# Sliding-window attention into a Silu MLP: first layers of tiles 0 and 1 in all eight PSUM banks, the Silu table loaded behind batch 1's Exp, batch 1's values in the scores' banks

## The chip, the cores and the metric

The kernel runs on one core of one Trainium2 chip. The metric is device time in microseconds (us) for one launch, the median of several runs. Before the change it is 298.0 us over 11 runs, which lie between 296.94 and 300.13.

TensorE (PE) multiplies, and its weight loads are shown as PEld; VectorE (DVE) and ScalarE (ACT) read its results from PSUM; GpSimd (POOL) issues nearly all loads here; SyncE (SP) issues the stores. PSUM has eight banks of 128 partitions by 512 float32 numbers.

## The reference, cut to what matters

```python
# q, k, v: (8, 8, 576, 64) = batch, heads, sequence, head size
scores = scale * np.matmul(q, k.transpose(0, 1, 3, 2))
rel = pos[:, None] - pos[None, :]
mask = (rel >= 0) & (rel < 64)
scores = np.where(mask, scores, -1e9)
attn = softmax(scores)                       # exp, divided by the sum over keys
x = matmul(attn, v), heads side by side      # (4608, 512)
h = x @ w_in                                 # (512, 2048)
g = h * (1.0 / (1.0 + np.exp(-h)))           # Silu
out = g @ w_out                              # (2048, 512), float32
```

A query sees only itself and the 63 keys before it, so a block of 64 queries needs a window of 128 keys. The largest score need not be subtracted at these sizes, and the kernel does not subtract it.

## The kernel before, in words

**Attention.** A batch has 576 positions, nine blocks of 64. Batch 0 is done in six units of three blocks and half of the heads. Batches 1 to 7 are done in *visits* of three blocks (four from batch 2's seventh block on) over all heads (`add_visit`, L570). A visit is a chain over four engines: scores on PE into the four banks called `at` (`scores`, L326), four Exps on ACT that free these banks (`expo`, L343), four multiplications by a 0/1 mask on DVE (`masking`, L346), the values product on PE (`values`, L362, called pv below) into two banks, and for each of these on DVE a reciprocal (`inverse`), a multiplication (`normal`) and a transpose into the tile `bridge` (`to_bridge`). `bridge` holds the attention's output with the model dimension on the partitions, as the MLP wants it.

**MLP.** The 4608 tokens are nine tiles of 512. A tile's first layer makes 16 stripes `ft` of 128 hidden units: four matmuls (`first_layer`, L392) into one bank, then one Silu on ACT into an SBUF tile `g` (`silu`, L398). The second layer (`second_layer`, L404) accumulates 16 stripes into one bank per 128 tokens, then copies the bank to SBUF (`copy_out`, L410) and stores it (`store`, L413). Tile 0 takes all nine blocks of batch 0, 64 tokens more than it needs; `rest_of_first` (L401) copies their stripes over to tile 1. Tile 0's second layer goes stripe by stripe over four banks, so that it can follow the stripes of `w_out` as they land; the other tiles finish one bank after the other. Tile 1's first layer comes in two parts for 14 of its stripes: 192 tokens (batch 1's first visit), then 256 tokens (its second and third).

**The order of work.** No scheduler of the compiler orders this kernel. `Plan.run` (L47) is a list scheduler that runs when the kernel is built: each operation is put in a queue by its class (`add`, L28) with an estimated duration, the operations that it depends on, and a latency `lat` after which its result counts as seen (0.08 us if none is given). At every simulated moment each free engine takes, among the heads of its queues, the ready one with the lowest rank: the class's number plus the batch, or a number of its own for batch 0 (`rank0`, and `ahead` for classes whose name ends in 0). The order that results is each engine's instruction order on the chip, where an engine waits at each instruction for what it needs. A load on POOL counts as seen at its transfer's modelled end plus `lat` plus 1.2 us; no more than eight are under way. All loads after the first few share one queue, in the order in which they were added.

**Banks.** An operation that opens a bank takes it from a pool (L176): `at` is banks 0 to 3, `mp` banks 4 to 7, `pv` banks 4 and 5, `all` all eight. A bank is free once the operations in its `untils` list are seen. An operation of the pools `at`, `pv` or `all` that is ready but finds too few free banks keeps its pool from operations of higher rank number. Before the change the first layers open their banks in `mp`, batch 1's first visit puts its values in `at` and its second and third in `pv`. The gate `scores_may_run` (L426) lets whole visits' scores in only while the next MLP matmul is of a second layer with enough left.

**Activation tables.** The plan starts with Exp's table and charges 1.28 us for a change. An operation of class `prime` (L688) does one small Silu as soon as batch 0's Exps are done, so that the table is there for tile 0.

## Time and profile before

| | |
|---|---|
| median of 11 runs | 298.0 us |
| profiled execution: its own time | 299.71 us |
| profiled execution: span, first to last instruction | 297.9 us |
| PE busy (matmuls) | 285.0 us, 96% |
| ACT busy | 169.2 us, 57% |
| DVE busy | 141.8 us, 48% |
| POOL busy | 117.8 us, 40% |
| granted TensorE clock | 1.000 of full speed, mean |

The profiled execution took 1.8 us more than its span and 1.7 us more than the median. Busy time is a sum over a program whose stages differ: loads fill the first 60 us or so (the page's DMA row is at 8 or 9 tenths there), and PE is busy at nearly every moment afterwards. So the stages have to be read one by one. In a line of the timeline the columns are start in us, length in us, engine, source line, operation, destination and sources, and how many instructions were merged; a bracket tells the idle time before it and what ended it. In the chain the columns are start, length and what the time went to; "issue" there is time for which the profile names no wait.

### The profile page before, as it was taken

How to read it: one execution, taken by the hardware profiler on the slowest of the kernel's cores; microseconds unless marked ns; L12 is line 12 of the kernel's file. 1: busy time of each engine (PE TensorE's matmuls, PEld its weight loads, DVE VectorE, ACT ScalarE, POOL GpSimd, SP SyncE). 2: the span in 40 equal slices, each digit the busy share in tenths (PEclk: the TensorE clock that was granted, in tenths of full speed). 3: DMA queues.
4: the chain of work that ended last, by engine and by line, in shares of the span. 5: the costliest groups of instructions: out<-in, count | busy, mean ns of one | idle time of the engine just before them, and what ended most of it. 6: DMA issues, size and time to landing. Idle time of an engine off the chain costs nothing.

```text
span 297.9 us, 8490 instructions
## 1 busy us (share of the span) xinstructions
PE 285.0 (96%) x3611; PEld 150.5 (51%) x3641; DVE 141.8 (48%) x344; ACT 169.2 (57%) x316; POOL 117.8 (40%) x175
## 2 busy tenths in 40 slices
PE   7989977899999999999999999999999999999996
PEld 4567633685444554455544554455544444444445
DVE  3872377868894687837792891065504000000000
ACT  4878654786387636773487447654863157126511
POOL 8967894969799997980320000000000000000000
PEclk9999999999999999999999999999999999999999
DMA  8999999999999999994290120011100210010012
GB/s 167 173 188 181 149 155 151 226 142 132 160 178 136 118 163 173 157 108 94 52 111 0 37 75 35 1 37 64 49 0 4 96 42 2 35 70 35 3 70 72
DMA packets 82982, 28.64 MB, mean 96 GB/s; under 512 B 72448, under 2 KB 78208, under 8 KB 82944
## 3 DMA queue, kind: packets, MB, share of 16 engines
q0 software_dynamic: 77184, 18.07, 65.7%
q1 hardware_dynamic: 5760, 10.03, 9.4%
q8 instruction: 28, 0.46, 0.6%
q14 instruction: 10, 0.08, 0.1%
HBM read 36.70 MB, written 9.44 MB: 155 GB/s over the span
## 4 chain that ended last, share of the span: by engine, by line
PE 80%; DMA 8%; POOL 7%; issue 3%; ACT 1%; POOLq 0%; ACTq 0%
PE mp L393 30%; PE mp L405 29%; PE at L405 9%; PE at L393 6%; DMA w_out_sb<-in_moe_w_out_dram 5%; PE mp L368 3%; DMA w_in_sb<-in_moe_w_in_dram 3%; PE at L334 3%; POOL vv L255 2%; POOL w_in_sb L261 2%; POOL nat L241 1%; POOL natb L231 1%; POOL w_out_sb L267 0%; ACT ot L411 0%; ACT g L399 0%
## 5 line engine op out<-in xcount | busy, mean ns | idle before, releaser
L393 PE MATMUL mp<-bridge,w_in_sb 128*128 128x512 bf16 (+5 forms) x612 | 109.9, 337 | 2.6 <-ACT g L399 0.8
L405 PE MATMUL mp<-w_out_sb,g 128*128 128x512 bf16 x421 | 97.4, 379 | 5.3 <-DMA w_out_sb<-in_moe_w_out_dram 2.6
L393 PEld LDWEIGHTS <-w_in_sb 128*128 128x128 bf16 x696 | 66.6, 98 | 61.7 <-issue 3.1
L399 ACT ACTIVATE g<-mp 128x512 bf16<-128x512 f32 (+5 forms) x153 | 77.4, 513 | 26.5 <-PE mp L393 25.3
L405 PEld LDWEIGHTS <-g 128*128 128x128 bf16 x608 | 56.5, 98 | 65.3 <-issue 3.5
L344 ACT ACTIVATE e<-at 128x512 bf16<-128x512 f32 (+1 forms) x68 | 33.0, 572 | 16.3 <-PE at L334 16.2
L241 POOL DMA_DIRECT2D nat<-in_k_dram x56 | 34.7, 633 | 13.8 <-DMA vv<-in_v_dram 6.5
L255 POOL DMA_DIRECT2D vv<-in_v_dram x32 | 32.0, 1018 | 14.1 <-PE mp L368 12.4
L411 ACT COPY ot<-mp 128x512 f32<-128x512 f32 x20 | 11.6, 587 | 44.8 <-PE mp L405 22.6
L241 POOL DMA_DIRECT2D nat<-in_q_dram x56 | 35.0, 644 | 2.9 <-DMA w_in_sb<-in_moe_w_in_dram 1.5
L375 DVE RECIPROCAL rc<-mp 128x6 f32<-128x6 f32 (+1 forms) x47 | 7.9, 185 | 49.4 <-PE mp L368 48.8
L405 PE MATMUL at<-w_out_sb,g 128*128 128x512 bf16 (+2 forms) x157 | 28.2, 336 | 0.2
L248 DVE STREAM_TRANSPOSE kt<-nat 128x576 bf16<-128x576 bf16 x28 | 20.7, 786 | 7.5 <-DMA nat<-in_k_dram 7.5
L349 DVE TENSOR_TENSOR e<-e,masks 128x512 bf16<-128x512 bf16 (+1 forms) x68 | 23.3, 392 | 1.5 <-ACT e L344 1.2
L248 DVE STREAM_TRANSPOSE qt<-nat 128x576 bf16<-128x576 bf16 x28 | 21.0, 792 | 3.8 <-DMA nat<-in_q_dram 3.7
L378 DVE TENSOR_TENSOR ox<-mp,rc 128x384 bf16<-128x384 f32 (+1 forms) x47 | 21.6, 510 | 0.1
L382 DVE STREAM_TRANSPOSE bridge<-ox 128x384 bf16<-128x384 bf16 x40 | 20.6, 552 | 0.0
L393 PE MATMUL at<-bridge,w_in_sb 128*128 128x512 bf16 x84 | 19.3, 379 | 0.0
L411 ACT COPY ot<-at 128x512 f32<-128x512 f32 (+2 forms) x10 | 5.0, 500 | 22.4 <-PE at L405 22.4
L399 ACT ACTIVATE g<-at 128x512 bf16<-128x512 f32 x21 | 12.5, 597 | 5.7 <-PE at L393 5.7
L301 DVE COPY vv<-vv 64x576 bf16<-64x576 bf16 (+1 forms) x14 | 7.3, 520 | 12.6 <-DMA vv<-in_v_dram 7.3
L368 PEld LDWEIGHTS <-e 128*32 128x32 bf16 x1008 | 9.6, 94 | 6.7 <-issue 5.8
(63 smaller groups left out, 138.1 us busy)
## 6 DMA issues: line engine op xcount, KB each, us to landing
out_dram<-ot SPq DMA_DIRECT2D x35, 256.0 KB, 2.4
vv<-in_v_dram POOLq DMA_DIRECT2D x32, 144.0 KB, 5.7
nat<-in_q_dram POOLq DMA_DIRECT2D x56, 72.0 KB, 4.0
nat<-in_k_dram POOLq DMA_DIRECT2D x56, 72.0 KB, 3.9
w_out_sb<-in_moe_w_out_dram POOLq DMA_DIRECT2D x8, 256.0 KB, 6.5
w_in_sb<-in_moe_w_in_dram POOLq DMA_DIRECT2D x6, 256.0 KB, 7.4
w_in_sb<-in_moe_w_in_dram POOLq DMA_DIRECT2D x4, 128.0 KB, 4.9
natb<-in_q_dram POOLq DMA_DIRECT2D x3, 144.0 KB, 5.2
```

What stands on the lines that cost most here:

```text
L241: nc.gpsimd.dma_start(out=nats[i][32 * h:32 * h + 32].rearrange("p (m x) -> p m x", m=NB), in_=(q, k)[kk][b, 4 * a + h].rearrange("(m p r) ...
L248: nc.vector.transpose(out=to[:, (2 * a + part) * S:(2 * a + part + 1) * S].rearrange("x (m t r) -> x m r t", t=32, r=2), in_=nats[i].rearr ...
L255: queue[e].dma_start(out=vv[b % NV][:, 2 * g0 + 1:2 * g1 + 1:2, 0:D], in_=v[b].rearrange("h s d -> (h s) d").rearrange("(g p) d -> p g d", ...
L344: nc.scalar.activation(out=es[e % NE][:, 0:128 * n], in_=banks[bank][:, 0:128 * n], func=ACTF.Exp, scale=scale)
L349: nc.vector.tensor_mul(at, at, masks[:, i:i + n].rearrange("k x h i -> k (x h i)"))
L368: nc.tensor.matmul(at_pv(bank)[32 * h:32 * h + 32, u, t], lhsT=es[(e + h) % NE][:, at:at + 32], rhs=vv[b % NV][:, (4 * a + h) * NB + i, 0: ...
L378: nc.vector.tensor_mul(oxs[n % NOX][:, 0:w], at_pv(bank)[:, 0:w, :, 0:D], rcs[n % NRC][:, 0:w].unsqueeze(3).to_broadcast([128, w, 2, D]))
L382: nc.vector.transpose(out=bridge[:, n0:n0 + w, 2 * a:2 * a + 2].rearrange("x t s (u i) -> x t s u i", u=2), in_=oxs[n % NOX][:, 0:w].rearr ...
L393: nc.tensor.matmul(banks[bank["bank"][0]][:, 0:hi - lo], lhsT=w_in_sb[:, c, ft * 128:(ft + 1) * 128], rhs=bridge[:, (j * TT + lo) // 64:(j ...
L399: nc.scalar.activation(out=gts[gt][:, lo:hi], in_=banks[bank["bank"][0]][:, 0:hi - lo], func=ACTF.Silu)
L405: nc.tensor.matmul(banks[bank["bank"][0]][:, 0:hi - lo], lhsT=gts[gt][:, m * 128:(m + 1) * 128], rhs=w_out_sb[:, f, lo:hi], start=(f == 0) ...
L411: copies[e](out=ots[ot][:, lo:hi], in_=banks[bank["bank"][0]][:, 0:hi - lo])
```

## The change

Seven edits, all in the plan; no instruction of the arithmetic changes.

1. Load estimates: loads of batch 0 that cast on the way (`load_first_cast`) and batch 0's v loads get `lat` 0.7 (they had 0.08 and 0); the w_in loads get 0.6 (first 512 columns) and 1.4 (0.08 before).
2. Batch 1's masks move to a class of their own, `mask1`, with rank -1.5 (its number with the batch is -0.5, the `mask` class had 2).
3. Batch 1's second and third visits put their values in the pool `at` instead of `pv`.
4. The reciprocal, multiplication and transpose of batch 1's first visit go to the classes of batch 0's first group (`inverse0`, `norm0`, `bridge0`), which stand ahead of everything else that DVE does then.
5. The first layers of tiles 0 and 1 open their banks in `all` instead of `mp`.
6. Tile 0's four output copies are done by ACT alone; they went to whichever of ACT and DVE was free.
7. A second `prime` loads Silu's table as soon as batch 1's twelve Exps are done.

```diff
+    CAL = 0.7
...
-        rank=dict(..., exp=1, mask=1, lift=2, ...),
+        rank=dict(..., exp=1, mask=1, mask1=-1.5, lift=2, ...),
...
-                ca = p.add("early" if ... else "dma0", {"POOL": 0.6}, lambda _, ...: load_first_cast(w, u, kk), dma=0.74)
+                ca = p.add("early" if ... else "dma0", {"POOL": 0.6}, lambda _, ...: load_first_cast(w, u, kk), dma=0.74, lat=CAL)
...
-            p.add("dma", {"POOL": 1.0}, lambda e, part=part: load_v(e, b, part), busy, dma=1.0 if b == 0 else 1.1, lat=MARGIN * (b > 0)) for part in parts)
+            p.add("dma", {"POOL": 1.0}, lambda e, part=part: load_v(e, b, part), busy, dma=1.0 if b == 0 else 1.1, lat=MARGIN if b else CAL) for part in parts)
...
             s["untils"][i].append(ex)
-            ready.append(p.add("mask", {"DVE": 0.37 + 0.1 * (w - 3)}, lambda _, i=i: masking(e + i, w, first), [ex, *c_mask], b=b))
+            exps.setdefault(b, []).append(ex)
+            ready.append(p.add("mask" if b > 1 else "mask1", {"DVE": 0.37 + 0.1 * (w - 3)}, lambda _, i=i: masking(e + i, w, first), [ex, *c_mask], b=b))
...
-                   pool="pv3" if b > 1 else "pv" if n > 6 else "at", b=b, nb=len(parts))
+                   pool="pv3" if b > 1 else "at", b=b, nb=len(parts))
...
-                add_bank(pv, i, len(units), lambda ...: to_bridge(n, at, a, k), range(at, at + len(units)), "", b)
+                add_bank(pv, i, len(units), lambda ...: to_bridge(n, at, a, k), range(at, at + len(units)), *(("0", 0) if at == NB else ("", b)))
...
                            have + win[ft] + (exps[0] if j == 0 else []), lat=0.1,
-                           pool=None if c else "mp")
+                           pool=None if c else "mp" if j > 1 else "all")
...
-                cp = p.add("out", {"DVE": 0.18 + (hi - lo) / 1000, "ACT": 0.18 + (hi - lo) / 1160},
+                cp = p.add("out", {"ACT": 0.18 + (hi - lo) / 1160, **({"DVE": 0.18 + (hi - lo) / 1000} if j else {})},
...
-        landed = [p.add("dma", {"POOL": 0.6}, lambda ...: load_w_in(a, lo, hi), dma=1.31 * (hi - lo) / 512)
+        landed = [p.add("dma", {"POOL": 0.6}, lambda ...: load_w_in(a, lo, hi), dma=1.31 * (hi - lo) / 512, lat=0.6 if hi <= 512 else 1.4)
...
-    p.add("prime", {"ACT": 0.2}, lambda _: nc.scalar.activation(out=spare, in_=zero, func=ACTF.Silu), [c_zero] + exps[0],
-          table="silu")
+    def load_silu(b):
+        p.add("prime", {"ACT": 0.2}, lambda _: nc.scalar.activation(out=spare, in_=zero, func=ACTF.Silu), [c_zero] + exps[b],
+              table="silu")
+
+    load_silu(0)
...
         add_batch_attention(b)
+        if b == 1:
+            load_silu(1)
```

## The prediction

> **What bounds the kernel now.** I read the page's busy slices first: PE is at 96%, and the slices that are not at 9 lie in the first 60 us and at the very end. Then I asked for PE's waits.

> ```profile
> PE mp L405 <- DMA w_out_sb<-in_moe_w_out_dram: 2.6, 3, 1.2
> PE mp L405 <- issue: 2.1, 13, 0.2
> PE mp L393 <- ACT g L399: 0.8, 1, 0.8
> PE mp L393 <- DMA w_in_sb<-in_moe_w_in_dram: 0.7, 1, 0.7
> PE mp L393 <- issue: 0.5, 1, 0.5
> PE mp L393 <- DVE bridge L382: 0.3, 1, 0.3
> ```

> The columns are the total in us, how often, and the longest. After a bounded start PE waits three times for w_out, once for a Silu, and for little else. The chain of what ended last, around the change, tells which of them count:

> ```profile
> 40.40 8.46 DMA w_out_sb<-in_moe_w_out_dram
> 48.86 0.04 issue
> 48.90 0.59 PE mp L405 x2
> 49.49 0.49 PE at L368 x43
> 49.98 0.16 issue
> 50.14 2.34 PE mp L405 x10
> 52.48 0.02 issue
> 52.50 1.07 ACT ot L411 x2
> 53.57 0.02 issue
> 53.59 0.10 ACT L399
> 53.69 1.20 issue
> 54.88 0.34 ACT g L399
> ```

> Up to 48.90 the chain is loads: tile 0's second layer cannot finish before the seventh stripe pair of w_out lands. From 48.90 on it is work: the last 16 matmuls of that layer, a pv, two output copies, the table load (its 1.28 us are the 0.10 and 1.20 behind the copies) and the first Silu of tile 1. PE's own timeline shows the same as holes:

> ```profile
> 47.12 0.59 PE L405 MATMUL mp<-w_out_sb,g 128*128 128x512 bf16 x2 [0.16 <-issue]
> 48.90 0.59 PE L405 MATMUL mp<-w_out_sb,g 128*128 128x512 bf16 x2 [1.19 <-DMA w_out_sb<-in_moe_w_out_dram]
> 49.42 0.56 PE L368 MATMUL at<-vv,e 128*32 128x65 bf16 x48
> 53.14 0.82 PE L393 MATMUL mp<-bridge,w_in_sb 128*128 128x192 bf16 x8
> 53.89 0.56 PE L368 MATMUL mp<-vv,e 128*32 128x65 bf16 x48
> 55.27 1.73 PE L393 MATMUL mp<-bridge,w_in_sb 128*128 128x192 bf16 x16 [0.82 <-ACT g L399]
> ```

> At 53.14 only two banks are to be had, two stripes fill them, and PE stands until the Silu at 54.88 has freed one. So there are three stages. Before 48.90 PE has slack (0.21, 1.16 and 1.19 us of w_out waits) and earlier work gains nothing. From 48.90 to 60.7 it is busy 10.62 of 11.80 us. From 68 to 284 it is busy 213.07 of 216.00, so what is won by 60.7 stays won, and nothing later is left to win.

> **The change part by part.**

> *Load estimates (edit 1).* No transfer moves: all these loads go through one POOL queue in the order in which they were added, and the only other work there (two selects for constants) still precedes the v loads. Cost 0 on the chip; the cover is the 2.56 us of w_out waits, and without it every 0.1 us of late start in tile 0 would be 0.1 us at the end. What the edit moves is the plan's idea of when batch 0 is ready, by 0.62 us (0.7 for 0.08), so its PE order meets the w_out estimates later. A few more warm-up matmuls (0.24 to 0.34 us each by the rows of L677) go in before 10 us; same cover.

> *Silu's table behind batch 1's Exps (edit 7).* It adds one small Silu of 0.20 us (the 0.205 us row of L688) and moves a load of 1.28 us. The last Exp ends at 47.01 + 1.64 = 48.65, and ACT then does one copy of 0.24 us and sits idle 2.88 us until 52.50; the load ends near 50.1, covered. Queued behind it is that copy, which nobody reads before tile 1's second layer at 68.5. Should the Exps end later than 51, the load is back on the path at up to 1.28 us. Gain: the table's share of PE's hole of 0.82 us.

> *Four copies on ACT (edit 6).* Two move from DVE (0.686 us each) to ACT (0.588): ACT does 4 x 0.588 = 2.35 us where it did 2 x 0.588 + 1.28 = 2.46. By itself this would leave the first Silu near 54.9 and the hole almost where it is. The four stores on SP's queue follow the copies up to 1.2 us later; the next use of their buffers is a copy at 72.23. Cost 0.

> *First layers in eight banks (edit 5).* This removes the hole. At tile 1's start the `at` banks hold no scores (the next ones come in the second layer, at 68.04), so stripes go there while ACT copies. A stripe of 192 tokens takes PE about 0.4 us (8 in 0.82), a Silu 0.33 us (two in 0.66), so a late start on ACT by two us costs five banks and is then made up. With the table the whole 0.82 us goes, and 0.11 more of the 0.93 idle in 53.1 to 57.4 at most. For tile 0 nothing is gained: its waits are for `bridge` and w_in (0.32, 0.70), and w_out hides them.

> *Values in `at` and masks ahead (edits 2, 3, 4).* The third visit's scores have left `at` by 48.65, so second and third pv can run inside tile 0's second layer, as soon as masks and banks allow, instead of at 53.89 and 56.93. They cost the same 0.49 us on PE. A pv ahead of a first layer shows no gap (57.00 + 0.49, then 57.48); ahead of a second-layer matmul the chain shows 0.16 at 49.98, and none at 80.55. So the move costs 0 to 0.16 for each of two, and I take half, 0.16 in all: rows of both kinds are about equally near. DVE gives the first visit's chain 0.42 + 0.98 + 1.03 us, ends it before 53, and has no copy of 1.29 in between; block transposes for batch 2 stand behind it and were done 3.6 us before their scores (64.42 against 68.04). Cost 0 from there.

> Sum from 48.90 on: -0.82 (hole) - 0.11 (the other idle) + 0.16 (gaps) = -0.77 us; bounds -0.93 and -0.50. On the profiled execution that is 299.71 - 0.77 = 298.94, and 1.71 less for the median of the runs: 297.2 us.

> [...]

> **The rivals.**

> *The first pv slips into the w_out wait.* In the trace it stands two matmuls behind the wait that ends at 48.90, and its last input, batch 1's last v block, is shifted by 48.30. If the plan, with batch 0 moved 0.62 us back against unmoved w_out estimates, puts it ahead of that wait, its 0.49 + 0.16 us vanish in the 1.19 hole: -0.65 more, 296.6. If the second pv comes with it, up to another 0.65: 295.9. For it: the distance is two matmuls, 0.43 us, less than the 0.62. Against: it must wait for two of the third visit's Exps to free banks, and these follow PE's order too, so part of the shift cancels.

> *The copies take the table's place.* With four copies in ACT's queue before any Silu, and `at` banks still held by pv results that DVE has not read, PE again has two banks at 53 and stands for 0.8: no gain, 298.0, or 298.3 with the gaps. For it: 2.35 against 2.46 us on ACT. Against: at least two `at` banks are past their norms by 52.

> *Scores behind Silus (slower).* Tile 1's last stripes may now sit in `at` banks, and batch 2's first scores need all four. The PE queue is in order: if the plan puts these scores where it believes the banks free, and ACT, which has 2.35 us of copies to make up and 0.41 to 0.55 us per Silu against 0.44 to 0.76 on PE, is late, PE stands. Each Silu that ACT is behind costs 0.55 us; it decides against the change from three on (1.65 less 0.77 gives +0.9), and with all four copies' 2.35 us left over the time is 298.0 - 0.77 + 2.35 = 299.6. For it: ACT was busy 12.19 of 14.90 us between 53.1 and 68. Against: in the trace ACT waits four times for PE between 55 and 59 (0.36, 0.25, 0.59, 0.25), so it catches up.

> *The slack before 48.90 is used up* or the third visit's scores land behind the wait: +0.55 + 0.16 against -0.77, about no change.

> **How the numbers follow.** About 0.3%, 0.9 us, is what a measurement of this kernel can tell from no change. Chances: the forecast 0.44, and since 0.50 to 0.93 lies around that limit, with later order shifting it by some tenths either way, 0.18 of it faster, 0.24 same, 0.02 slower; the pv in the wait 0.30, of it 0.29 faster and 0.01 same; copies for table, or scores behind the wait, 0.08, half same and half slower by a reshuffled later order; scores behind Silus, or a like stop in a reordered later tile, 0.18, of it 0.16 slower and 0.02 same. In all faster 0.47, same 0.31, slower 0.22. The range goes from the two pvs in the wait (295.9) to 298.9, which cuts the slow case at its lower half.

> **What would show it.** Right: a table load of 1.28 us on ACT near 49, four copies on ACT and then Silu without a load; L393 written to `at` from 53 on and no wait of PE for a Silu there; two or three pvs before tile 1's first L393; tile 1's 256-token part, at 60.3 before, 0.5 to 0.9 us earlier, and all later stages by as much. The last w_out wait still ends near 48.9. Wrong: that wait ending more than half a us elsewhere (loads are not fixed, then), a wait of PE ahead of scores at 67 to 69, or PE idle over 3.5 us between 68 and 284.

## The result, and the profile after

The changed kernel takes 300.68 us in the median of 12 runs (298.9 to 302.41), against 297.77 us for the kernel before in the same comparison (47 runs). The ratio is 1.0093, 95% interval [1.0073, 1.0113]: slower by 2.9 us in the medians, above the range, and on the other side of the forecast. The changed kernel's source has one line more above the functions, so that L393, L405, L368 and L334 of before are L394, L406, L369 and L335 here.

First PE's waits in the profiled execution of the changed kernel (299.64 us, span 297.9); the columns are total us, how often, and the longest:

```profile
PE mp L406 <- issue: 2.9, 18, 0.2
PE at L369 <- issue: 2.7, 1, 2.7
PE mp L394 <- DMA w_in_sb<-in_moe_w_in_dram: 1.7, 1, 1.7
```

The w_out waits, 2.6 us in the view of before, are gone. So is the wait for a Silu. In their place stands one wait of 2.7 us on L369, the values product, and it is put down to "issue": PE waits, and the profile names nothing that it waits for. The chain of what ended last shows its place:

```profile
48.00 0.49 PE at L369 x42
48.49 0.16 issue
48.65 0.38 PE mp L406
49.02 0.42 PE at L369 x37
49.45 2.69 issue
52.13 0.25 PE at L369 x8
...
52.54 2.32 PE mp L406 x10
54.86 0.49 PE at L369 x48
```

All three of batch 1's values products now stand inside tile 0's second layer, as the forecast had it for two of them. Between the first and the second lie only two second-layer matmuls with their weight loads (48.49 to 49.02; the trace holds a record of the second of them alone). PE's timeline shows that the second product is cut in two:

```profile
47.93 0.56 PE L369 MATMUL at<-vv,e 128*32 128x65 bf16 x48
48.65 0.38 PE L406 MATMUL mp<-w_out_sb,g 128*128 128x512 bf16 x1 [0.16 <-issue]
48.95 0.49 PE L369 MATMUL at<-vv,e 128*32 128x65 bf16 x40
52.13 0.25 PE L369 MATMUL at<-vv,e 128*32 128x65 bf16 x8 [2.69 <-issue]
...
56.15 0.49 PE L394 MATMUL at<-bridge,w_in_sb 128*128 128x192 bf16 x4
56.48 0.49 PE L394 MATMUL mp<-bridge,w_in_sb 128*128 128x192 bf16 x4
```

After 40 of its 48 matmuls PE stands for 2.69 us, and then does the other 8. Data cannot be what these 8 lack: by DVE's rows in the same trace this visit's last mask ended at 46.37 and the last copy of batch 1's v blocks at 47.10, and by ACT's the last Exp that frees a bank ended at 48.51. From 56.15 on stripes go alternately to `at` and `mp`. ACT's timeline in the same execution:

```profile
48.52 1.28 ACT L691 ACT_TABLE_LOAD   x1
...
55.71 1.07 ACT L412 COPY ot<-mp 128x512 f32<-128x512 f32 x2 [5.40 <-PE at L369]
56.68 0.33 ACT L400 ACTIVATE g<-at 128x192 bf16<-128x192 f32 x1
```

The table is loaded at 48.52 and covered, and the first Silu follows the copies without a load. ACT then waits 5.40 us for PE.

What the stop can be waiting for shows in the DMA view of the stretch from 49.4 to 52.2 of the same execution (queue, kind: packets, MB, share of 16 engines):

```profile
q0 software_dynamic: 1645, 0.40, 148.0%
q8 instruction: 1, 0.02, 2.1%
```

One transfer of 16 KB came through the queue of kind "instruction", in the middle of 1645 packets of the kernel's own loads. By the trace it ran from 49.81 to 50.76. The page counts 28 of them in the execution, 0.46 MB. PE has 3645 weight loads and as many matmuls, 7290 instructions, or 260 for each of the 28 transfers, and the counts below go in steps of 256, so I take the queue to be PE's. In four profiled executions that show the stop whole, the same transfer and the same place go together:

| execution | transfer of 16 KB | PE goes on | stop | after |
|---|---|---|---|---|
| changed kernel, first | 49.81 to 50.76 | 52.13 | 2.69 | 40 of 48 |
| changed kernel, `again` | 49.35 to 50.39 | 51.72 | 1.83 | 40 of 48 |
| changed kernel, `again2` | 50.94 to 51.87 | 53.25 | 2.84 | 40 of 48 |
| without edit 1, `no1` | 50.16 to 51.10 | 52.48 | 1.75 | 42 of 48 |

In all four the trace holds 735 weight loads of PE up to the stop, so it is the same count of instructions each time (`no1`, below, has two matmuls fewer ahead of that product, and stops two matmuls further into it), and PE goes on 1.3 to 1.4 us after the landing. In the kernel before the same transfer came at 49.76 to 50.70 and at 49.21 to 50.14 in two executions, when PE had begun only 689 and 695 weight loads: there the dense values products lay apart, and PE, as I read it, had not yet got to the end of what it had.

The counts show the size of the block too. The twelve profiles of this case, the experiments' included, hold twelve waits of PE of over 0.3 us that are put down to "issue". They stand after 351, 735, 1631, 1759 or 2143 weight loads, and these differ by whole multiples of 128 loads, which with their matmuls are 256 instructions. Each ends 1.26 to 1.55 us after a transfer of 16 KB on that queue has landed.

A second thing is seen not in this profile but over the executions: the granted clock, averaged over one execution, is 0.993 or 0.994 in 7 of the 12 runs of the changed kernel and 1.000 in the others, and the median span is 299.8 us in the former and 297.9 in the latter. Of the kernel before, 3 of 69 executions in the later comparisons were under 0.998.

### The profile page after: what moved, and what is told of

The parts are those of the page before. It is cut to its first block, busy times and chain, and to the rows that moved or that the text cites. A ratio compares the mean times of both kernels' runs of the same rounds, so it can differ in the third digit from the quotient of the medians.

```text
span 297.9 us, 8482 instructions
## 1 busy us (share of the span) xinstructions
PE 284.6 (96%) x3611; PEld 150.8 (51%) x3645; DVE 141.0 (47%) x341; ACT 169.8 (57%) x320; POOL 118.9 (40%) x175
## 4 chain that ended last, share of the span: by engine, by line
PE 83%; POOL 7%; DMA 5%; issue 3%; DVE 1%; ACT 0%; POOLq 0%; DVEq 0%; ACTq 0%
PE mp L406 31%; PE mp L394 28%; PE at L406 9%; PE at L394 9%; PE at L335 3%; DMA w_in_sb<-in_moe_w_in_dram 3%; PE mp L369 3%; POOL w_in_sb L262 2%; DMA nat<-in_k_dram 2%; POOL nat L242 2%; POOL vv L256 1%; POOL natb L232 1%; PE at L369 1%; DVE kt L249 1%; POOL w_out_sb L268 0%
## 5 line engine op out<-in xcount | busy, mean ns | idle before, releaser
L406 PE MATMUL mp<-w_out_sb,g 128*128 128x512 bf16 x417 | 96.6, 379 | 3.5 <-issue 2.9
L394 PE MATMUL mp<-bridge,w_in_sb 128*128 128x512 bf16 (+5 forms) x464 | 96.0, 358 | 1.7 <-DMA w_in_sb<-in_moe_w_in_dram 1.7
L394 PEld LDWEIGHTS <-w_in_sb 128*128 128x128 bf16 x696 | 66.6, 98 | 60.0 <-DMA w_in_sb<-in_moe_w_in_dram 2.1
L406 PEld LDWEIGHTS <-g 128*128 128x128 bf16 x608 | 56.4, 98 | 61.9 <-issue 0.2
L400 ACT ACTIVATE g<-mp 128x512 bf16<-128x512 f32 (+5 forms) x116 | 63.4, 556 | 23.3 <-PE mp L394 22.9
L242 POOL DMA_DIRECT2D nat<-in_k_dram x56 | 35.7, 660 | 9.9 <-DMA nat<-in_q_dram 3.4
L412 ACT COPY ot<-mp 128x512 f32<-128x512 f32 x22 | 12.8, 587 | 45.8 <-issue 24.3
L394 PE MATMUL at<-bridge,w_in_sb 128*128 128x512 bf16 (+5 forms) x232 | 38.8, 310 | 0.0
L256 POOL DMA_DIRECT2D vv<-in_v_dram x32 | 32.8, 1040 | 14.9 <-PE mp L369 13.9
L400 ACT ACTIVATE g<-at 128x512 bf16<-128x512 f32 (+5 forms) x58 | 26.2, 460 | 7.2 <-PE at L394 6.7
L406 PE MATMUL at<-w_out_sb,g 128*128 128x512 bf16 (+2 forms) x157 | 28.2, 336 | 0.2
L379 DVE TENSOR_TENSOR ox<-mp,rc 128x384 bf16<-128x384 f32 (+1 forms) x45 | 20.5, 508 | 0.2
L369 PEld LDWEIGHTS <-e 128*32 128x32 bf16 x1008 | 9.6, 94 | 10.0 <-issue 8.7
L335 PE MATMUL at<-qt,kt 32*128 32x64 bf16 x1008 | 11.4, 191 | 0.7 <-DVE kt L249 0.5
```

The source lines that it names most:

```text
L242: nc.gpsimd.dma_start(out=nats[i][32 * h:32 * h + 32].rearrange("p (m x) -> p m x", m=NB), in_=(q, k)[kk][b, 4 * a + h].rearrange("(m p r) ...
L256: queue[e].dma_start(out=vv[b % NV][:, 2 * g0 + 1:2 * g1 + 1:2, 0:D], in_=v[b].rearrange("h s d -> (h s) d").rearrange("(g p) d -> p g d", ...
L335: nc.tensor.matmul(banks[op["bank"][h]][:, (2 * x + a) * 64:(2 * x + a + 1) * 64], lhsT=kt[b % NK][r, at:at + 128], rhs=qt[b % NK][r, at:a ...
L369: nc.tensor.matmul(at_pv(bank)[32 * h:32 * h + 32, u, t], lhsT=es[(e + h) % NE][:, at:at + 32], rhs=vv[b % NV][:, (4 * a + h) * NB + i, 0: ...
L379: nc.vector.tensor_mul(oxs[n % NOX][:, 0:w], at_pv(bank)[:, 0:w, :, 0:D], rcs[n % NRC][:, 0:w].unsqueeze(3).to_broadcast([128, w, 2, D]))
L394: nc.tensor.matmul(banks[bank["bank"][0]][:, 0:hi - lo], lhsT=w_in_sb[:, c, ft * 128:(ft + 1) * 128], rhs=bridge[:, (j * TT + lo) // 64:(j ...
```

## The experiments

**The theory (F) and its rivals.** F: the second values product stands almost directly behind the first, so PE uses up some 180 instructions in 1.5 us, the next block of instructions comes late through queues full of loads, and PE stands until it is there; what is lost after that is clock. The rivals: the load estimates (edit 1) start tile 0 later, and that is all of it; the order after tile 1 is a worse one (table, banks); the stop is a wait for data or banks that the profile fails to name.

**The change once more, against the kernel before.** No edit.

> The changed kernel once more, for a second profile and the clocks of its runs. Theory F (instruction fetch): PE stops in the middle of the second pv without any named wait, as it did for 2.69 us at 49.45 in the first profile, because scores, pv and pv of batch 1, three groups of 96 short instructions, follow each other within 3.2 us while the next 16 KB block of PE's instructions is still under way on the instruction queue; so a stop of 2 to 3 us at the same instruction, and a ratio of 1.006 to 1.011. Theory L (loads): the stop is chance and the loss is the later start of tile 0 (its first layer stood 1.69 us for w_in, against 0.70 before); then no stop at that instruction here, but again a late tile 0. Theory C (clock): the granted clock is below 1 in most runs (0.994 in seven of the first twelve, worth 0.6% of 285 us = 1.7 us), and the profile's span at clock 1.000 is about that of the kernel before.

301.05 us, ratio 1.0113 [1.0071, 1.0154]. The stop is there again (1.83 us, after 40 matmuls), a little shorter than expected, and the ratio a little higher; 3 of 6 executions are below 0.998 of the clock. The result repeats, and the stop does. Tile 0 is late here too (1.7 us of waits for w_in), so this run alone does not part the theories.

**The second values product held back.** All seven edits; the second visit's values are let in only when tile 0's second layer is done, and the third's stand behind them in the same queue:

```diff
+        held = [moe[-1][0]] if blocks[0] == (1, 3) else []
...
-        pv = p.add("pv", {"PE": 0.1 + 0.147 * w}, None, ready + [d for b in all_b ...], lat=0.1,
+        pv = p.add("pv", {"PE": 0.1 + 0.147 * w}, None, ready + held + [d for b in all_b ...], lat=0.1,
```

> The changed kernel with the second visit's values held until tile 0's second layer is through, so that second and third pv lie in tile 1's first layer, as before the change; all seven edits stay. Theory F: no stop of PE over 0.5 us between 46 and 60, the gains stay: ratio to the kernel before 0.991 to 0.998 (295.1 to 297.2 us), about 2.5 us under the changed kernel. Theory L: as slow as the changed kernel, within 0.5 us, as the start is the same. Theory C: clock below 1 as often as in the changed kernel and a ratio above 1.003.

297.47 us, ratio 0.9995 [0.9976, 1.0015]: the loss of 1.0 to 1.1% is gone. The longest of PE's waits in this kernel:

```profile
PE mp L406 <- DMA w_out_sb<-in_moe_w_out_dram: 1.5, 2, 1.3
```

No stop on L369, and the w_out waits are back. Two of 12 executions are under 0.998 of the clock. So the dense stretch is worth about 1% by itself, and what is left of the seven edits is a draw. That misses the 0.991 to 0.998 that theory F expected: something else costs what the other edits win.

**Edit 1 alone.** The kernel before with the four changed estimates (`lat=CAL` for batch 0's casting loads and v loads, 0.6 and 1.4 for w_in).

> The kernel before with edit 1 alone (the estimates of the first loads); it puts the first pv ahead of the w_out wait and leaves banks, copies, table and the other two pvs. Theory F: no stop in mid-pv; the first pv's 0.65 us go into the wait, the Silu hole of 0.8 stays: 0.996 to 1.001. Theory L: the later start is due to this edit (more warm-up matmuls, batch 0 reordered), so the loss of 2 to 3 us shows here: 1.006 to 1.010. Theory C: clock as in the kernel before, 1.000.

298.81 us, ratio 1.0053 [1.003, 1.0076]: edit 1 does cost, between what the theories F and L expected. The loads kept their order (the first issue of w_in is 0.4 us later, 9.75 against 9.37), but PE's order at the start changed. First the last unit of batch 0 in another execution of the kernel before (`before_again`, below), then in the held kernel that has edit 1; L313 and L314 open a bank of scores, L355 and L356 are values products, L393 and L394 tile 0's first layer:

```profile
13.64 0.56 PE L355 MATMUL at<-vv,e 128*32 128x65 bf16 x48
14.03 0.40 PE L355 MATMUL mp<-vv,e 128*32 128x65 bf16 x24
14.36 0.34 PE L313 MATMUL mp<-bias,ident 128*128 128x384 bf16 x1
...
16.28 0.37 PE L355 MATMUL mp<-vv,e 128*32 128x65 bf16 x22 [0.17 <-ACT e L341]
16.58 0.34 PE L393 MATMUL mp<-bridge,w_in_sb 128*128 128x192 bf16 x2
```

```profile
13.72 0.78 PE L356 MATMUL mp<-vv,e 128*32 128x65 bf16 x72
14.84 0.21 PE L356 MATMUL at<-vv,e 128*32 128x65 bf16 x2 [0.34 <-ACT e L342]
15.22 0.36 PE L356 MATMUL at<-vv,e 128*32 128x65 bf16 x22 [0.17 <-ACT e L342]
15.52 0.50 PE L314 MATMUL at<-bias,ident 128*128 128x384 bf16 x2
...
17.25 0.36 PE L356 MATMUL mp<-vv,e 128*32 128x65 bf16 x22 [0.17 <-ACT e L342]
17.55 1.49 PE L394 MATMUL at<-bridge,w_in_sb 128*128 128x192 bf16 x16
```

With edit 1 the last unit's scores stand behind 24 more values matmuls and behind two waits for Exps (0.34 and 0.17), start 1.16 us later (15.52 against 14.36), and tile 0's first layer starts 0.97 us later. In the profile of edit 1 alone it starts 2.2 us later (18.77), and the w_out waits are gone: they were the cover, and they are used up. That these two profiles show how the 0.5% comes about is a reading; no run changed this order alone.

**Edit 7 alone.** The kernel before with the second `prime`.

> The kernel before with edit 7 alone (Silu's table loaded behind batch 1's Exps). By the prediction's own working the hole of 0.82 us in front of tile 1's third stripe shrinks, and PE then has two banks until the first Silu: 0.997 to 1.000. All theories of the loss expect no stop in mid-pv, since the second pv stays in tile 1's first layer; F expects it for that reason, L because the start of the kernel is untouched, C a clock of 1.000.

297.75 us, ratio 1.0015 [0.9994, 1.0035]: no difference that can be told, where 0.997 to 1.000 was expected. The wait for the first Silu is gone, but tile 1's first layer is hardly shorter: from its first L393 to tile 1's first L405 it takes 15.3 us (52.32 to 67.6), against 15.4 in `before_again` (51.78 to 67.2). The groups of PE in these two stretches, `before_again` first:

```profile
L393 PE MATMUL mp<-bridge,w_in_sb 128*128 128x192 bf16 (+2 forms) x120 | 13.1, 265 | 1.0 <-ACT g L399 0.8
```

```profile
L393 PE MATMUL mp<-bridge,w_in_sb 128*128 128x192 bf16 (+2 forms) x120 | 13.6, 265 | 0.5
```

The idle time falls by 0.5 us (1.0 to 0.5, the last column) and the busy time rises by as much, so with four banks PE gains at most 0.1 us there in these two profiles. The hole of 0.82 was a symptom of that stage, not its price.

**The kernel before once more, for a profile.** No edit.

> The kernel before once more, for a second profile: the first profiled execution (span 297.9) lay 1.9 us above the median span of 29 later executions (295.7). Expected: span 295 to 296.5, clock 1.000, no stop of PE in mid-pv, tile 2's first L393 between 82.5 and 84 (84.76 in the first profile), so that tile for tile the profiles can be set against those of the other runs.

297.75 us, span 296.0, which is what the runs of before show in the median, where its first profile (299.71, span 297.9) was longer by 1.7. PE's waits:

```profile
PE mp L405 <- DMA w_out_sb<-in_moe_w_out_dram: 1.2, 2, 1.1
...
PE mp L393 <- ACT g L399: 0.8, 1, 0.8
```

The w_out slack is 1.2 us here, not 2.6. Against this execution the first profile of the changed kernel can be balanced at the start of tile 2's first layer, 85.32 against 83.40, so +1.92 us: the stop +2.69; tile 0's second layer starts 0.94 later (35.08 against 34.14); w_out waits -1.2; hole -0.82; waits for batch 1's keys ahead of its first scores +0.5 (L335 for `kt`, in the view of after alone); together +2.1, which leaves 0.2 unexplained. From there to the last instruction both take 212.6 us.

**The stop moved.** In the changed kernel each warm-up matmul of PE is split into two of 192 columns, which computes nothing else and puts 50 more instructions, 25 weight loads and 25 matmuls, ahead of the place.

```diff
-        nc.tensor.matmul(banks[op["bank"][0]][:, 0:384], lhsT=blank, rhs=blank.unsqueeze(1).to_broadcast([128, 3, 128]), ...)
+        for lo in (0, 192):
+            nc.tensor.matmul(banks[op["bank"][0]][:, lo:lo + 192], lhsT=blank, rhs=blank[:, 0:64].unsqueeze(1).to_broadcast([128, 3, 64]), ...)
```

> The changed kernel with each warm-up matmul of 384 columns issued as two of 192: same columns, 50 more PE instructions (25 weight loads, 25 matmuls) ahead of everything, nothing else. Theory F, if the stop sits where PE has used up the instructions delivered so far: the same count is reached 25 matmuls earlier, so PE stops about 15 matmuls into the 48 of the second pv instead of 40, some 0.3 us earlier, and the stop is longer by that, 2.0 to 3.0 us; time as the changed kernel or up to 0.5 us more. Rival: the stop belongs to the operands of those eight matmuls (a bank or an unnamed wait); then it stays ahead of the last eight.

301.35 us, ratio 1.0102 [1.0072, 1.0132]. PE's timeline:

```profile
52.32 0.30 PE L369 MATMUL at<-vv,e 128*32 128x65 bf16 x15
53.38 0.43 PE L369 MATMUL at<-vv,e 128*32 128x65 bf16 x33 [0.76 <-issue]
```

The stop comes after 15 matmuls of the same product: 40 less the 25 that were put ahead. Data, banks and masks are the same; what has moved is the count of instructions. The trace again holds 735 weight loads up to the stop. This excludes a wait for data that the profile fails to name. The stop is short here, 0.76 us instead of the 2 to 3 expected, since an earlier wait had put PE back; the time is not better, and all 8 executions were at a clock below 0.998. That earlier wait, on tile 0's first matmul, is named after `bridge`, and the windows of core 0 around it show where this execution lost its clock (from and to, and length, in us; busy time and instructions of PE, PEld, DVE, ACT, POOL; granted clock; DMA share; GB/s):

```profile
21.73 2.72 PE L394 MATMUL at<-bridge,w_in_sb 128*128 128x192 bf16 x16 [3.77 <-DVE bridge L383]
```

```profile
18.00:22.00 4.00, 0.27 (x2) 0.25 (x2) 3.88 (x9) 1.06 (x2) 0.93 (x2) 0.59 1.19 191
22.00:26.00 4.00, 4.00 (x30) 3.71 (x28) 0.00 (x0) 1.90 (x6) 1.99 (x3) 0.55 1.43 192
```

The two transposes that this matmul needs had ended at 17.82. It stands after 351 weight loads and went on 1.64 us after a transfer of 16 KB had landed (19.20 to 20.09), so its numbers fit a stop of the same kind under another name; no run tests that. Behind the stop in the values product the clock of this execution is 1.00 (50 to 58).

**The loads held away.** In the changed kernel batch 2's first load waits on POOL until the second values product is done, so that the instruction transfer meets fewer loads.

```diff
+        if b == 2:
+            second = next(op for op in p.queues["pv"] if op.get("b") == (1, 3))
+            p.add("dma", {"POOL": 0.1}, lambda _: nc.gpsimd.memset(es[4][:, 0:2], 0.0), [second])
...
+        pv["b"] = blocks[0]
```

> The changed kernel with one POOL operation ahead of batch 2's first load that waits for the second pv, so that no load of batch 2 is in flight until then (seven are issued between 42 and 50 in the changed kernel); all else the same. Theory F with its queueing half (the block of instructions comes late because the transfer engines are full of loads): the block of 16 KB lands at 46.5 to 48.5 instead of 50.8, the stop shrinks below 1 us or goes, and the time falls to 296 to 299 us. If the block is late for another reason, or stuck behind w_out alone, the stop stays at 1.5 to 3 us and the time at 300 us or more.

298.57 us, ratio 1.0024 [0.9999, 1.0049]. PE's timeline:

```profile
50.34 0.52 PE L369 MATMUL at<-vv,e 128*32 128x65 bf16 x40
51.53 0.24 PE L369 MATMUL at<-vv,e 128*32 128x65 bf16 x8 [0.68 <-issue]
```

The stop is at the same instruction and only 0.68 us long, and some 0.8% of time is back. The transfer (49.31 to 50.26) did not land at 46.5 to 48.5, as expected. The reading is not clean: in this profile tile 0's second layer started 2.2 us later than in the first profile of the changed kernel (37.28), and PE reached the place later. Measured from the point 128 weight loads ahead of the stop, which PE passed at 47.75, the transfer began 1.56 us later here, and 2.3 to 3.6 us later in the other eleven profiles. It took 0.95 us, as it did with the loads around it: if the loads matter, then by when it starts, not by how long it takes, and that rests on one execution. The half clock of this execution (0.994) lies at 22.6 to 26.0 (eight 128x384 matmuls from 22.56 on took 2.76 us, and four from 26.84 on 0.81), behind waits of PE for `bridge` and w_in of 0.66 and 1.55 us, and not behind this stop.

**The changed kernel once more, for a profile.** No edit.

> The changed kernel a third time, one look, for a profile with a granted clock below 1 (10 of its 18 executions so far had 0.988 to 0.994). Expected of theory F: the stop at the same eight matmuls again. Expected of the clock as a consequence of the stop: if the mean clock is below 1, the slice after the stop is the one with the low clock, and the stop is longer than the 2.69 and 1.83 us of the two profiles at 1.000; expected if the low clock has another cause: a low slice elsewhere.

302.64 us, span 300.8, clock 0.994. Here the lower clock can be seen in its place. The windows of core 0 (columns as above):

```profile
52.00:54.00 2.00, 0.59 (x10) 0.43 (x11) 0.46 (x2) 0.00 (x0) 1.69 (x4) 1.00 1.45 137
54.00:56.00 2.00, 2.00 (x7) 0.74 (x5) 0.17 (x1) 0.00 (x0) 2.00 (x4) 0.50 1.21 120
56.00:58.00 2.00, 2.00 (x53) 0.73 (x51) 0.00 (x0) 0.00 (x0) 2.00 (x3) 0.65 1.18 113
```

and PE's timeline:

```profile
53.25 0.25 PE L369 MATMUL at<-vv,e 128*32 128x65 bf16 x8 [2.84 <-issue]
53.65 4.01 PE L406 MATMUL mp<-w_out_sb,g 128*128 128x512 bf16 x10 [0.16 <-issue]
```

The stop was 2.84 us, and behind it the clock fell to 0.50: ten matmuls that took 2.32 us behind the stop of 2.69 took 4.01. That is 1.7 us more, which is about the difference of 1.9 between the two kinds of executions of the changed kernel. By the windows the half clock lasted about 3.4 us, 54.0 to 57.4 (2 us at 0.50, and 0.7 of the next 2 us, which makes 0.65 there). Ahead of it, with the stop, PE was busy 0.59 of the 2 us from 52 to 54. It was so in some executions and not in others: in the first profile of the changed kernel the mean clock is 1.000 with a stop of 2.69 us. What sets the clock down is not shown. Of the three profiles below 1 that were taken of versions with the stop, this is the only one in which the low clock lies behind it. That the stop costs clock in most of the others too is argued from counts: where the second product stands close behind the first (the changed kernel and `no1`, below), 18 of 31 executions are under 0.998; in the kernel before, the two versions that hold the product back, edit 1 alone and edit 7 alone, it is 7 of 117.

This profile has a second stop of the same kind, in tile 0's first layer, after 351 weight loads:

```profile
22.35 0.41 PE L394 MATMUL at<-bridge,w_in_sb 128*128 128x192 bf16 x3 [1.06 <-issue]
```

**Edits 2 to 7, without edit 1.**

> Edits 2 to 7 without the load estimates of edit 1. PE's order is then: the third visit's scores, ten instructions of tile 0's second layer, the first values product (96 instructions), two, the second values product (96), twenty-four, the third (96). So the second values product still stands almost directly behind the first. Theory F (PE runs out of fetched instructions there) expects a stop of 1 to 3 us in or right behind the second values product for which the profile names no wait, behind a transfer of the instruction queue that lands 1.3 to 1.5 us before PE goes on, unless the w_out wait ahead of the first product (about 1.2 us in before) gives the transfer its time; a time of 0.998 to 1.008 of before. If edit 1 is the whole cause (the plan's lateness, not the fetch), there is no stop and the time is 0.995 to 1.000 of before.

299.48 us, ratio 1.0047 [1.0017, 1.0077]. Its order has two matmuls fewer than the changed kernel's ahead of the second product. PE's timeline:

```profile
49.41 0.56 PE L368 MATMUL at<-vv,e 128*32 128x65 bf16 x48
50.22 0.52 PE L368 MATMUL at<-vv,e 128*32 128x65 bf16 x42 [0.25 <-issue]
52.48 0.24 PE L368 MATMUL at<-vv,e 128*32 128x65 bf16 x6 [1.75 <-issue]
```

The stop is there without edit 1, after 42 matmuls instead of 40, which is the same count from the start, and 7 of 12 executions were at a clock of 0.993 or 0.994. Edit 1 is not the whole cause. Against the changed kernel (1.0093 and 1.0113) it is 0.5 to 0.7% better: that is edit 1's part.

**Edits 2 to 7 without edit 1, and the second values product held back.** The two lines of the held kernel, without those of edit 1.

> Edits 2 to 7 without edit 1, and the second visit's values held until tile 0's second layer is done, as in the run that held them with all seven edits. Then neither the dense stretch of values products nor the moved estimates are there. If the loss of the change is the fetch stop plus edit 1 (which alone gave 1.005), this is the best of the versions: no stop without a named wait, tile 1 without the hole behind the first Silu, 0.993 to 0.998 of before. If edit 1 costs nothing inside the change, it is the same as the held version, 0.9995 (0.998 to 1.001). If something else in edits 2 to 7 loses time later on, it is above 1.002.

296.33 us, ratio 0.9949 [0.9921, 0.9977]: faster than both kernels, by 1.5 us against the one before. Of PE's waits, those in second layers:

```profile
PE mp L405 <- issue: 2.4, 15, 0.2
...
PE mp L405 <- DMA w_out_sb<-in_moe_w_out_dram: 0.5, 1, 0.5
```

and its timeline at the place:

```profile
47.90 0.56 PE L368 MATMUL at<-vv,e 128*32 128x65 bf16 x48
48.62 2.97 PE L405 MATMUL mp<-w_out_sb,g 128*128 128x512 bf16 x13 [0.16 <-issue]
...
51.68 0.56 PE L368 MATMUL at<-vv,e 128*32 128x65 bf16 x48
```

Between the two values products 2.97 us of large matmuls give the 16 KB their time (48.76 to 49.69 in this trace); no execution of the 12 was below 0.998 of the clock. This is what was expected but for one thing: a stop put down to "issue" is left, 0.56 us at 21.31 in tile 0's first layer, after 351 weight loads.

**What the runs add up to.** Edit 1 and the second product were each measured in two or three places, each difference to 0.2 to 0.4%, and the places agree:

| part | from | in % of the time before |
|---|---|---|
| edit 1 | alone 1.0053; in the held kernel 0.9949 to 0.9995; in the change 1.0047 to 1.0093 | +0.5 in each |
| second values product close behind the first | 0.9995 to 1.0093; without edit 1, 0.9949 to 1.0047 | +1.0 in each |
| the other edits | 0.9949 [0.9921, 0.9977] without both | -0.5 |
| sum | | +1.0, measured +0.9 and +1.1 |

The sum is no check of its own: 0.9949, the 0.46 of edit 1 in the held kernel and the 0.98 of the second product lead to 1.0093 by subtraction. What stands by itself is that edit 1 costs as much alone as inside the change, and that the second product costs as much without edit 1 as with it.

The times fit. For the last 128 weight loads ahead of the stop, and their matmuls, PE took 3.1 us in the changed kernel (46.37 to 49.45 in its first profile), but it went on only 4.9 to 5.9 us after the start of that stretch. In the best version PE took 5.5 us for the same 128 (46.34 to 51.88) and did not stop. Open is what decides when the block is asked for, and what PE does between its landing and the next matmul.

## Why the prediction was wrong

*Values in `at`: "They cost the same 0.49 us on PE."* This is the step that failed. The second product took from 48.95 to 52.38, 3.43 us instead of 0.49: PE stopped in its middle for 2.69 us, after 735 weight loads, and went on 1.37 us after a transfer of 16 KB on the instruction queue had landed; I read this as PE out of instructions. The executions at a lower clock, over half of them, took about 1.9 us more, and one profile shows that clock right behind the stop. I priced a group of small matmuls by its own row wherever it stood, with 0 to 0.16 us for the gap; the rows that I had all showed such groups between large matmuls. By the two pairs above the term is +1.0% or 2.9 us, not 0 to 0.16. The 0.16 itself was nothing: in `again`, whose trace has a record of all 3645 matmuls, there is no such gap, while the executions that show it have 3611 or so; it is a second-layer matmul whose record is missing.

*Load estimates: "Cost 0 on the chip; the cover is the 2.56 us of w_out waits."* Wrong by 0.5%, 1.4 us. The loads kept their order, as forecast, though not their times to the last 0.4 us. But I looked for the effect on PE's order only near the w_out estimates and in a few warm-up matmuls, and not in batch 0 itself, where the last unit's scores went behind values products and start 1.16 us later. And the cover was read from an execution that was 1.7 us longer than the median: in one of usual length it is 1.2 us. That tile 0 could start later without loss holds for the first of these, not for what came.

*Silu's table and eight banks: "With the table the whole 0.82 us goes."* The hole went, by either way, and the load is covered as forecast (48.52 to 49.80). As a gain the hole was mis-sized for the table alone: 0.1 us in its stage. With banks as well, in the best version, tile 1's first layer takes 14.3 us (51.42 to 65.7) against 15.4 before, although one second-layer matmul more lies in it. Edits 2 to 7 less the dense stretch won 1.5 us, 0.7 to 2.4 by the interval, so the forecast 0.77 cannot be told from it; the direction was right, and no run parts the banks from the other edits.

*Four copies on ACT.* Only two stand ahead of the first Silu (55.71); the other two come at 63.44 and 67.37 between Silus. No cost is seen from them. Their stores and buffers did not show.

*The rivals.* The first one came: the first values product stands ahead of the last w_out wait, and no such wait is left. What that alone brings is not shown: edit 1 alone also moves it there and also starts tile 0 later, and is slower. "Scores behind Silus", the case I had for slower, did not come: from 56.15 to 68.4 PE has no wait. The true slower case, PE short of instructions, was not among them, although the profile of before shows 28 transfers on its instruction queue, and although one of the rows above is such a stop: the 0.5 us of "issue" on L393 are 0.46 us at 118.26, after 1759 weight loads.

## What to carry to other kernels

Moving a group of many tiny matmuls next to another was not free here (+1.0%), though the data of both had come: after some 180 instructions in 1.5 us PE stood for 2.69 us in the first profile, until 1.37 us after the next 16 KB had landed, while with 3 us of large matmuls between the same two groups it did not stop there. An estimate in a list scheduler is a change of order everywhere before the place that it was meant for, so its cost is found by comparing the whole instruction order, not by asking which transfer moves. And read a cover (a wait that is to hide a delay) from an execution whose time is near the median: here one profile showed 2.6 us of it and the next 1.2.

## What the runs showed of the hardware

In `again2` a stop of 2.84 us was followed by half the clock for about 3.4 us (0.50 in one window of 2 us; 0.65 in the next, so 0.7 of it), and in the first profile one of 2.69 was not; the mean over the execution is then 0.994, and the median span of such executions 1.9 us longer (299.8 against 297.9). In `warm_split` an early wait of 3.77 us went with half the clock from 18.8 to 25.6 (0.59 and 0.55 in the two windows of 4 us) and a mean of 0.989, so a low mean alone does not tell where the clock was lost.

The gaps of 0.16 us ahead of a large matmul behind a group of small ones were missing records here: the groups there count one matmul less than the program (1 of 2 at 48.65 in the first profile, with 3611 records), and `again`, with all 3645, shows 2 at 48.86 and no gap.
